# Regrouping the tokens of a fused agent-attention and feed-forward kernel: 26 pairs of 480-token groups become 24 pairs of 512 and one pair of 192

## The chip, the cores and the metric

The kernel runs on one core of one Trainium2 chip. A core has a matrix engine (TensorE, PE in the profile; its weight loads are PEld), a vector engine (VectorE, DVE), a scalar engine (ScalarE, ACT), GpSimd (POOL) and a queue engine that issues transfers (SyncE, SP). The metric is the device time of one execution in microseconds (us), lower is better.

## The reference, cut to what matters

```python
B, N, C = 2, 12480, 128;  n_agents = 49;  d_ff = 2048
def sm(a, b):                                   # softmax over b's rows
    s = (a @ b.T) / sqrt(C); e = exp(s - s.max(-1)); return e / (e.sum(-1) + 1e-9)
agent_v = sm(agents, k) @ v                     # per batch: 49 x 128
x = sm(q, agents) @ agent_v                     # per batch: 12480 x 128
h = x @ w_in                                    # 24960 x 2048
out = (max(h, 0) + alpha * min(h, 0)) @ w_out   # 24960 x 128
```

All data are float32 (the weights arrive as float64 words, which the kernel narrows).

## The kernel before, in words

The kernel never forms `x`. For each batch it folds `agent_v @ w_in` into one table `sab` (a high part `sa` and a low part `sb`, 49 agents padded to 64 rows, kept twice, once in each half of the 128 partitions) and works with the unnormalized softmax weights `qmh` + `qml` (high and low part) of each query. A product of two float32 values is built of three float32r passes (high with low, low with high, high with high).

`PReLU(h)` is split into a linear part and a ReLU part: the ReLU part runs over all 2048 columns of `d_ff`, and the linear part `alpha * h @ w_out` is folded into a 128 x 128 matrix `wz`, and with `agent_v` into `zh` + `zl` per batch.

**Groups and steps.** Tokens are taken in groups of GT = 480, 26 per batch, 52 in all. A group has NM = 8 steps, each of 256 columns of `d_ff`, so there are 416 steps. Step s consists of
- `g1`: h = sab.T @ (qmh, qml), 6 matmuls of 64 rows and 480 columns into one of two PSUM buffers; then on ScalarE `rh = relu(h)` and on VectorE `rl = max(h, 0) - rh`;
- `g2`: acc += wl.T rh + wh.T rh + wh.T rl, 12 matmuls of 64 rows and 480 columns.

Each matmul uses one half of the array's rows (`TILES`, rows 0 to 63 or 64 to 127), and the two halves work side by side, each in its own order. I call the time that one half takes for one matmul a *slot*: a step is 9 slots. After the last step of a group come three linear passes with `zh` and `zl` (line 854), one on the first half and two on the second, and then `os` (ScalarE copies one half of acc, VectorE adds the other), `ot` (a transposition on VectorE), `ot` times `qr` (the softmax denominators) and the store, 8 steps later.

**What sets the order.** The whole order is written out: at step s the loop (line 1118) emits first what `pre` put there, then `g1(s + 2)`, then what `at` put there, then `g2(s)`. Each engine works through its own list in that order. So `g1(s + 2)` may start only when `rl(s)` has freed the PSUM buffer, and everything that stands on VectorE ahead of an `rl` delays it.

**Beside the steps** runs, for each pair of groups, the query chain `q_chain` (load, transposition, split in high and low, logits `lg` of 6 slots, maximum over the agents on GpSimd, exponential, split, `qsum` of 2 slots, reciprocal). And while the first batch's groups run, the second batch's keys and values are worked off: `k_transpose_dve`, `k_logits` (`kl`, matmuls of 49 columns), `k_max_keys`; then `k_exp_a` (line 507, VectorE), `k_exp_b` (ScalarE), `k_exp_c` (line 526, VectorE), `v_split` (line 498, VectorE), `k_av2` (`av`, matmuls of 258 columns) and `k_add` (line 582, VectorE); and then `fold_tasks`: `den`, `avt`, four tasks `ta` (`a_ps`, 512 columns of `sab` each; one float32 matmul leaves two records), `tz` and `ts`, which make `zh` and `zl`. Their places are found by a planner: `fit` looks for a step in which the sum of VectorE or ScalarE costs stays under `ROOM` (1.4 and 1.1), and `hold` for one in which the misc PSUM buffer is free. A prologue of some 86 us does the first batch's keys and values and narrows the weights.

Of the kernel before, what the change touches and what calls it, by code (L numbers as in the profile page):

```python
# [20 lines left out]
ROOM = {"dve": 1.4, "act": 1.1}  # L21
# [4 lines left out]
SLAB_PARTS = (0, 0, 0, 1, 2, 3, 5, 6, 7, 10)  # L26
# [5 lines left out]
def kernel(  # L32
# [19 lines left out]
    GT = 480  # L52
    TB = GT // 32
    NG = N // GT
    KT = 512
# [10 lines left out]
    assert N % GT == 0 and N % 64 == 0 and NA <= HALF and C == P and D == P and DFF % W == 0  # L66
# [194 lines left out]
    def narrow_wo(n):  # L261
# [328 lines left out]
    def fold_tasks(b):  # L590
# [38 lines left out]
        def ta(n):  # L629
            def f():  # L630
                t = pair_tile(f"a_ps{b}_{n}", 0 if b == 0 and n == 1 else None)[:, 0, :]
                sl = slice(n * W, (n + 1) * W)
                nc.tensor.matmul(t, lhsT=w["avt"], rhs=win[:, sl], start=True, stop=True)
                nc.scalar.copy(out=w["sa"][:, sl], in_=t)
                nc.vector.tensor_tensor(
                    out=w["sb"][:, sl], in0=t, in1=w["sa"][:, sl], op=ALU.subtract
                )

            return f
# [13 lines left out]
        first = [t1, t2] + [ta(n) for n in range(4)]  # L653
# [45 lines left out]
    NGT = B * NG  # L699
    gq = {}  # L700

    def q_load(k):
        t = p2.tile([P, 2, TB, 32], F32, tag="qin", name=f"qin{k}")
        for i in range(2):
            b, r0 = (2 * k + i) // NG, (2 * k + i) % NG * GT
            view = q[b, r0 : r0 + GT, :].rearrange("(t j) (h b i) -> h b j t i", j=32, h=2, b=2)
            for h in range(2):
                for c in range(2):
                    p0 = HALF * i + 32 * c
                    nc.sync.dma_start(out=t[p0 : p0 + 32, h], in_=view[h, c])  # L710
        gq["in", k] = t
# [16 lines left out]
    def q_lo(k):  # L728
        t = p1.tile([P, 2, GT], F32R, tag="ql", name=f"ql{k}")
# [30 lines left out]
    def q_exp_hi(k):  # L760
        m = p2.tile([P, 2, GT], F32R, tag="qmh", name=f"qmh{k}")
# [7 lines left out]
    def q_split(k):  # L769
        m = p2.tile([P, 2, GT], F32R, tag="qml", name=f"qml{k}")  # L770
# [29 lines left out]
    def q_rec(k):  # L800
        t = p1m.tile([P, 32], F32, tag="qst", name=f"qst{k}")
        nc.vector.transpose(out=t, in_=gq.pop(("sum", k)))
        r = p2.tile([P, 2, TB, 1], F32, tag="qr", name=f"qr{k}")
        nc.vector.tensor_scalar(
            out=r.rearrange("p h t o -> p (h t o)"), in0=t[:, 0 : 2 * TB], scalar1=1e-9, scalar2=None, op0=ALU.add
        )
        nc.vector.reciprocal(out=r, in_=r)
        for i in range(2):
            gq["r", 2 * k + i] = r[:, i]
# [4 lines left out]
    def g1(s):  # L814
        g, m = divmod(s, NM)
        w, (mh, ml) = st[g // NG], gq["M", g]
        h = ps_h.tile([P, 2, 512], F32, tag="h", name=f"h{s}")
# [3 lines left out]
        for n, (a, x) in enumerate(jobs):  # L821
            for u, (r0, r1) in enumerate(TILES):
                f0 = (2 * m + u) * P
                nc.tensor.matmul(  # L824
                    h[:, u, 0:GT], lhsT=w[a][r0:r1, f0 : f0 + P], rhs=x[r0:r1, :],
                    start=n == 0, stop=n == 2,
                )
        rh = p3.tile([P, 2, GT], F32R, tag="rh", name=f"rh{s}")
        rl = p3.tile([P, 2, GT], F32R, tag="rl", name=f"rl{s}")
        nc.scalar.activation(out=rh, in_=h[:, :, 0:GT], func=AF.Relu)  # L830
        nc.vector.scalar_tensor_tensor(  # L831
            out=rl, in0=h[:, :, 0:GT], scalar=0.0, in1=rh, op0=ALU.max, op1=ALU.subtract
# [3 lines left out]
    def g2(s):  # L836
        g, m = divmod(s, NM)
        w = st[g // NG]
# [321 lines left out]
```

## Time and profile before

| what | value |
|---|---|
| median of 3 runs | 1036.88 us (1036.82 to 1041.66) |
| the profiled execution | 1039.85 us |
| its span, first to last instruction | 1038.1 us |
| TensorE busy / weight loads busy | 98% / 90% |
| VectorE / ScalarE / GpSimd busy | 79% / 61% / 11% |
| granted TensorE clock, mean | 0.994 of full speed |

The profiled execution took 1.75 us more than its span. A busy TensorE is not one that streams without gaps: records of two matmuls overlap, so the pace is read from the distance of their starts. The span has four stages: the prologue to 88.8 us, the keys of the second batch to 339.9 us, its values and the fold to 606.6 us, and then only groups and query chains.

### The profile page before, as it was taken

The page shows a single profiled execution, that of the slowest core. Times are in us where ns is not written, and L with a number is a line of the kernel's source. Part 1 is how long each engine was busy: PE and PEld are TensorE (multiplying, and loading weights), DVE is VectorE, ACT ScalarE, POOL GpSimd, SP SyncE. Part 2 cuts the span into 40 slices and gives each one's busy share as a digit, 9 for nine tenths or more (in the row PEclk, how much of TensorE's full clock was granted, in tenths as well). Part 3 has the DMA queues.
Part 4 walks back from the last instruction along what each step waited for, and adds up shares of the span by engine and source line. Part 5 has one row for each costly group of instructions (what it writes and reads, how often), then busy time and mean ns, then how long its engine had stood idle before and what let it go on. Part 6 is the DMA issues. An engine that isn't in the chain of part 4 may idle for free.

```text
span 1038.1 us, 22309 instructions
## 1 busy us (share of the span) xinstructions
PE 1018.8 (98%) x9263; PEld 936.6 (90%) x9263; DVE 818.6 (79%) x1040; ACT 630.8 (61%) x801; POOL 114.7 (11%) x138
## 2 busy tenths in 40 slices
PE   8999999999999999999999999999999999999997
PEld 7877888988999898999988799999999999999996
DVE  6776778878878899988976777787778877887775
ACT  4365656656655676776755666666656665666563
POOL 2260111011011011011011011101110011101100
PEclk9899999999999999999999999999999999999999
DMA  9963124333331232332210211121112120211011
GB/s 298 289 131 50 21 46 67 51 51 61 51 56 30 61 71 51 75 76 63 52 31 11 39 30 26 25 40 30 33 18 39 31 36 16 39 30 21 12 20 30
DMA packets 295045, 57.22 MB, mean 55 GB/s; under 512 B 265567, under 2 KB 292769, under 8 KB 294945
## 3 DMA queue, kind: packets, MB, share of 16 engines
q1 hardware_dynamic: 293953, 55.69, 26.8%
q8 instruction: 72, 1.18, 0.5%
q10 hardware_dynamic: 992, 0.12, 0.1%
q14 instruction: 28, 0.23, 0.1%
HBM read 42.59 MB, written 12.78 MB: 53 GB/s over the span
## 4 chain that ended last, share of the span: by engine, by line
PE 79%; DVE 13%; ACT 3%; DMA 3%; issue 2%; SPq 1%; DVEq 0%; ACTq 0%
PE acc L846 44%; PE h L824 23%; DVE rl L831 4%; PE lg L740 3%; PE kl L384 3%; ACT rh L830 2%; PE av L539 2%; PE acc L854 2%; DVE qt L718 1%; PE qsum L782 1%; DVE mx L423 1%; DVE ql L730 1%; DMA qin<-in_q_dram 1%; DMA win<-in_moe_w_in_dram 1%; DMA v<-in_v_dram 1%
## 5 line engine op out<-in xcount | busy, mean ns | idle before, releaser
L831 DVE SCALAR_TENSOR_TENSOR rl<-h,rh 128x960 fp32r<-128x960 f32 x416 | 478.7, 1152 | 186.5 <-ACT rh L830 182.9
L830 ACT ACTIVATE rh<-h 128x960 fp32r<-128x960 f32 x416 | 404.7, 973 | 286.8 <-PE h L824 277.8
L824 PE MATMUL h<-qmh,sab 64*128 64x480 f32 x1664 | 446.7, 381 | 4.1 <-DVE rl L831 3.3
L846 PE MATMUL acc<-rh,wl 64*128 64x480 f32 x1664 | 442.9, 380 | 1.2 <-DVE zl L649 0.7
L846 PE MATMUL acc<-rh,wh 64*128 64x480 f32 x1664 | 440.4, 377 | 0.0
L846 PE MATMUL acc<-rl,wh 64*128 64x480 f32 x1664 | 369.5, 378 | 0.0
L824 PEld LDWEIGHTS h<-qmh,sab 64*128 64x128 f32 x1664 | 252.2, 184 | 22.4 <-DVE rl L831 9.3
L846 PEld LDWEIGHTS acc<-rh,wl 64*128 64x128 f32 x1664 | 250.6, 184 | 17.1 <-issue 3.8
L846 PEld LDWEIGHTS acc<-rh,wh 64*128 64x128 f32 x1664 | 251.8, 184 | 10.2
L846 PEld LDWEIGHTS acc<-rl,wh 64*128 64x128 f32 x1664 | 247.3, 184 | 11.5
L824 PE MATMUL h<-qml,sab 64*128 64x480 f32 x832 | 254.3, 377 | 0.0
L753 POOL PARTITION_ALL_REDUCE qm<-qs x26 | 79.6, 3063 | 716.2 <-ACT qs L748 696.3
L824 PEld LDWEIGHTS h<-qml,sab 64*128 64x128 f32 x832 | 134.2, 185 | 4.8
L859 ACT COPY os<-acc 128x480 f32<-128x480 f32 x52 | 29.1, 560 | 40.8 <-PE acc L854 40.8
L384 PEld LDWEIGHTS kl<-ag,kt 64*128 64x128 f32 (+2 forms) x588 | 50.8, 193 | 2.2 <-ACT s L513 0.6
L384 PE MATMUL kl<-ag,kt 64*128 64x49 f32 (+2 forms) x588 | 51.4, 272 | 0.2 <-ACT kt L356 0.2
L860 DVE TENSOR_TENSOR os<-acc,os 128x480 f32<-128x480 f32 x52 | 33.6, 646 | 2.4 <-ACT os L859 2.4
L725 ACT CAST qh<-qt 128x960 fp32r<-128x960 f32 x26 | 25.9, 997 | 14.5 <-DVE qt L718 14.5
L865 DVE STREAM_TRANSPOSE ot<-os 128x480 f32<-128x480 f32 x52 | 34.7, 666 | 0.0
L870 DVE TENSOR_TENSOR ot<-ot,qr 128x480 f32<-128x480 f32 x52 | 33.6, 647 | 0.0
L404 ACT COPY s<-kl 128x196 f32<-128x196 f32 (+2 forms) x38 | 14.1, 370 | 29.0 <-PE kl L384 29.0
L748 ACT COPY qs<-lg 128x960 f32<-128x960 f32 x26 | 25.0, 960 | 10.4 <-PE lg L740 10.4
(148 smaller groups left out, 894.6 us busy)
## 6 DMA issues: line engine op xcount, KB each, us to landing
qin<-in_q_dram SPq DMA_DIRECT2D x208, 60.0 KB, 2.2
out_dram<-ot SPq DMA_DIRECT2D x206, 60.0 KB, 1.9
v<-in_v_dram SPq DMA_DIRECT2D x12, 512.0 KB, 8.0
kb<-in_k_dram SPq DMA_DIRECT2D x96, 64.0 KB, 2.2
v<-in_v_dram SPq DMA_DIRECT2D x24, 256.0 KB, 2.8
k<-in_k_dram SPq DMA_DIRECT2D x11, 512.0 KB, 8.4
win<-in_moe_w_in_dram SPq DMA_DIRECT2D x4, 512.0 KB, 8.0
wo<-in_moe_w_out_dram SPq DMA_DIRECT2D x4, 512.0 KB, 9.5
```

Of the source, the lines that this page charges most:

```text
L384: nc.tensor.matmul(d[0:rows, c : c + NA], lhsT=kt[r0:r1, n * rows : (n + 1) * rows], rhs=st[b]["ag"][r0:r1, 0:NA], start=True, stop=True,)
L725: nc.scalar.copy(out=t, in_=gq["t", k])
L740: nc.tensor.matmul(t[:, i, 0:GT], lhsT=a[r0:r1, h].rearrange("p d a -> p (d a)"), rhs=x[r0:r1, h, :], start=n == 0, stop=n == len(jobs) - 1,)
L753: nc.gpsimd.partition_all_reduce(flat(t), flat(gq["s", k]), P, ReduceOp.max)
L824: nc.tensor.matmul(h[:, u, 0:GT], lhsT=w[a][r0:r1, f0 : f0 + P], rhs=x[r0:r1, :], start=n == 0, stop=n == 2,)
L830: nc.scalar.activation(out=rh, in_=h[:, :, 0:GT], func=AF.Relu)
L831: nc.vector.scalar_tensor_tensor(out=rl, in0=h[:, :, 0:GT], scalar=0.0, in1=rh, op0=ALU.max, op1=ALU.subtract)
L846: nc.tensor.matmul(acc[:, i, 0:GT], lhsT=a[r0:r1, 2 * m + u, :], rhs=x[r0:r1, u, :], start=m == 0 and n == 0, stop=False,)
L859: nc.scalar.copy(out=t, in_=acc[:, 0, 0:GT])
L860: nc.vector.tensor_tensor(out=t, in0=acc[:, 1, 0:GT], in1=t, op=ALU.add)
L865: nc.vector.transpose(out=t.rearrange("p t i -> p (t i)"), in_=oo.pop(g))
L870: nc.vector.tensor_tensor(out=t, in0=t, in1=gq.pop(("r", g)).to_broadcast([P, TB, 32]), op=ALU.mult)
```

## The change

Groups have 512 tokens: 24 per batch, 48 in all. The 192 tokens that are left of each batch are two more groups, which form one last pair (the first of that pair belongs to batch 0, the second to batch 1). There are 50 groups and 400 steps instead of 416: 384 of 512 columns and 16 of 192. Tiles are cut to each pair's width by `pair_of`.

The three linear passes of a group put two on the second half for even groups, as before, and two on the first half for odd ones.

The second batch's keys start 3 steps earlier (`base + 5`), the planner's limits are 1.46 and 1.15, and its work has to be done in 16 steps fewer, since the first batch has 192 steps instead of 208. The four `ta` of the second batch become two tasks of two. In the prologue the tasks of `narrow_wo` move by a step (`SLAB_PARTS`) and `part` has one buffer.

```diff
-ROOM = {"dve": 1.4, "act": 1.1}
+ROOM = {"dve": 1.46, "act": 1.15}
-SLAB_PARTS = (0, 0, 0, 1, 2, 3, 5, 6, 7, 10)
+SLAB_PARTS = (0, 0, 0, 1, 2, 3, 5, 7, 7, 9)
...
-    GT = 480
+    GT = 512
     NG = N // GT
+    REST = N - NG * GT
...
-            part = x["part"] = p_tmp.tile([P, q4, D], F32, tag="part", name=f"part{n}", bufs=2)
+            part = x["part"] = p_tmp.tile([P, q4, D], F32, tag="part", name=f"part{n}", bufs=1)
...
-        def ta(n):
+        def ta(*ns):
...
+                for t, n in enumerate(ns):
+                    sl = slice(n * W, (n + 1) * W)
+                    nc.tensor.matmul(
+                        ps[:, t, :], lhsT=w["avt"], rhs=win[:, sl], start=True, stop=True
+                    )
+                    nc.scalar.copy(out=w["sa"][:, sl], in_=ps[:, t, :])
...
-        first = [t1, t2] + [ta(n) for n in range(4)]
+        whole = [(0, 1), (2, 3)] if b else [(n,) for n in range(4)]
+        first = [t1, t2] + [ta(*ns) for ns in whole]
...
-    NGT = B * NG
+    groups = [(b, g * GT, GT) for b in range(B) for g in range(NG)]
+    groups += [(b, NG * GT, REST) for b in range(B)]
+    NGT = len(groups)
...
+    def pair_of(pool, tag, k, dt=F32):
+        n = groups[2 * k][2]
+        t = pool.tile([P, 2 * GT], dt, tag=tag, name=f"{tag}{k}")[:, 0 : 2 * n]
+        return t.rearrange("p (h n) -> p h n", h=2)
...
-            for i, a, x in ((0, "zh", mh), (1, "zl", mh), (1, "zh", ml)):
+            jobs = ((0, "zh", mh), (1, "zl", mh), (1, "zh", ml))
+            if g % 2:
+                jobs = ((0, "zl", mh), (1, "zh", mh), (0, "zh", ml))
+            for i, a, x in jobs:
...
-            at(base + 8, k_begin, b, [(0, NU)], parts)
-            s = base + 9
+            at(base + 5, k_begin, b, [(0, NU)], parts)
+            s = base + 6
```

What moves is shown at three places. In all three, `name<-names` is what a row writes and reads; numbers after a name are the step, group or pair, then the buffer.

**First place: VectorE, where `zl` of the second batch stands** (`ot` is the scaling of an output group, `os` its sum, `rl` the step's own work). Before:

```order
L831 SCALAR_TENSOR_TENSOR rl209_7930<-h209_7922,rh209_7929 128x960
L870 TENSOR_TENSOR ot24_7760<-ot24_7760,qr12_7787 128x480
L649 TENSOR_TENSOR zl1_7935<-z_ps1_7908,zh1_7934 128x128
L860 TENSOR_TENSOR os25_7953<-acc25_7734,os25_7953 128x480
L831 SCALAR_TENSOR_TENSOR rl210_7964<-h210_7956,rh210_7963 128x960
```

And now:

```order
L853 SCALAR_TENSOR_TENSOR rl200_7666<-h200_7658,rh200_7665 128x1024
L774 TENSOR_TENSOR qs13_7573<-qs13_7573,qm13_7586 128x1024
L853 SCALAR_TENSOR_TENSOR rl201_7692<-h201_7684,rh201_7691 128x1024
L897 TENSOR_TENSOR ot23_7523<-ot23_7523,qr11_7309 128x512
L654 TENSOR_TENSOR zl1_7697<-z_ps1_7670,zh1_7696 128x128
L886 TENSOR_TENSOR os24_7715<-acc24_7499,os24_7715 128x512
L853 SCALAR_TENSOR_TENSOR rl202_7726<-h202_7718,rh202_7725 128x1024
```

Before, `zl1` stood ahead of the sum of group 25, the last group of the first batch, which does not read it; the first group that reads it, group 26, ended 8 steps later. Now it stands ahead of the sum of group 24, which is the first group of the second batch and reads it.

**Second place: VectorE at the values of the second batch** (steps 124 to 126; `qst`, `qr` reciprocal of the denominators, `s1` is `k_exp_a`, `e2` is `k_exp_c`, `v2` is `v_split`, `x1` is `k_add`). Before:

```order
L831 SCALAR_TENSOR_TENSOR rl124_5079<-h124_5071,rh124_5078 128x960
L802 STREAM_TRANSPOSE qst7_5082<-qx7_4893 128x32
L804 TENSOR_SCALAR qr7_5084<-qst7_5082 128x30
L807 RECIPROCAL qr7_5084<-qr7_5084 128x30
L507 TENSOR_TENSOR s1_1363<-s1_1363,kmax1_1365 128x196 x2
L582 TENSOR_TENSOR x1_1366<-av1_2_5097,x1_1366 98x516
L831 SCALAR_TENSOR_TENSOR rl125_5142<-h125_5134,rh125_5141 128x960
L771 TENSOR_TENSOR qml8_5145<-qs8_4824,qmh8_5049 128x960
L526 TENSOR_TENSOR e2_1_4_5114<-s1_1363,e2_1_4_5114 128x4x49
L831 SCALAR_TENSOR_TENSOR rl126_5174<-h126_5166,rh126_5173 128x960
```

And now:

```order
L853 SCALAR_TENSOR_TENSOR rl124_5081<-h124_5073,rh124_5080 128x1024
L822 STREAM_TRANSPOSE qst7_5084<-qx7_4893 128x32
L824 TENSOR_SCALAR qr7_5086<-qst7_5084 128x32
L828 RECIPROCAL qr7_5086<-qr7_5086 128x32
L526 TENSOR_TENSOR e2_1_4_5054<-s1_1284,e2_1_4_5054 128x4x49
L498 TENSOR_TENSOR v2_1_5_5117<-v1_5_4877,v2_1_5_5117 128x4x128
L582 TENSOR_TENSOR x1_1287<-av1_2_5099,x1_1287 98x516
L853 SCALAR_TENSOR_TENSOR rl125_5145<-h125_5137,rh125_5144 128x1024
L787 TENSOR_TENSOR qml8_5148<-qs8_4822,qmh8_5050 128x1024
L526 TENSOR_TENSOR e2_1_5_5121<-s1_1284,e2_1_5_5121 128x4x49
L853 SCALAR_TENSOR_TENSOR rl126_5179<-h126_5171,rh126_5178 128x1024
```

Here a `v2` and an `e2` moved into a step that had two `s1`; at step 126 the values are one block further on than before.

**Third place: TensorE, where `sab` of the second batch is made** (`a_ps` is `ta`). Before:

```order
L824 MATMUL h192_7427<-qml12_7357,sab0_1049 128x480 x2
L824 MATMUL h192_7427<-qmh12_7286,sab0_1049 128x480 x2
L633 MATMUL a_ps1_0_7440<-win_89,avt1_7387 128x512
L846 MATMUL acc23_7262<-rh190_7378,wl_95 128x480 x2
L846 MATMUL acc23_7262<-rh190_7378,wh_94 128x480 x2
```

And now:

```order
L846 MATMUL h190_7365<-qml11_6856,sab0_1049 128x512 x2
L846 MATMUL h190_7365<-qmh11_6762,sab0_1049 128x512 x2
L635 MATMUL a_ps1_0_7378<-win_89,avt1_7325 128x512 x2
L869 MATMUL acc23_7256<-rh188_7303,wl_95 128x512 x2
L869 MATMUL acc23_7256<-rh188_7303,wh_94 128x512 x2
```

Four interruptions by one matmul of the whole array became two by two matmuls.

## Rows read from the trace of the kernel before

**Rows 1.** The page, busy time, share of the span and instructions of each engine.

```profile
PE 1018.8 (98%) x9263; PEld 936.6 (90%) x9263; DVE 818.6 (79%) x1040; ACT 630.8 (61%) x801; POOL 114.7 (11%) x138
```

**Rows 2.** Three stages: stretch, length, busy time and count per engine, clock, DMA.

```profile
88.80:339.90 251.10, 249.23 (x2410) 221.39 (x2408) 198.17 (x236) 145.27 (x163) 21.78 (x14) 1.00 0.29 47
339.90:606.60 266.70, 263.32 (x2414) 232.05 (x2414) 226.39 (x307) 178.63 (x243) 25.19 (x40) 1.00 0.25 52
606.60:1014.10 407.50, 407.50 (x3715) 399.62 (x3713) 314.27 (x347) 254.79 (x274) 34.34 (x23) 1.00 0.17 28
```

**Rows 3.** Timeline of ScalarE, last stage, one row per pair of groups: start, length.

```profile
723.46 1.00 ACT L725 CAST qh<-qt 128x960 fp32r<-128x960 f32 x1 [0.51 <-DVE qt L718]
...
757.52 1.00 ACT L725 CAST qh<-qt 128x960 fp32r<-128x960 f32 x1 [0.51 <-DVE qt L718]
```

**Rows 4.** Timeline of TensorE at the end of a group, two linear passes.

```profile
710.87 0.37 PE L854 MATMUL acc<-qmh,zl 64*128 64x480 f32 x1
...
711.08 0.37 PE L854 MATMUL acc<-qml,zh 64*128 64x480 f32 x1
```

**Rows 5.** Timeline of TensorE, 512-column matmuls in the prologue, all eight and the first two.

```profile
64.33 2.11 PE L160 MATMUL stoke_max<-wh 128*128 128x512 f32 x8
...
64.33 0.73 PE L160 MATMUL stoke_max<-wh 128*128 128x512 f32 x2
```

**Rows 6.** Timeline of TensorE, narrower matmuls of 64 rows.

```profile
159.41 1.97 PE L384 MATMUL kl<-ag,kt 64*128 64x49 f32 x31
...
431.62 0.64 PE L572 MATMUL av<-v,e 64*98 64x258 f32 x8
```

**Rows 7.** Weight loads by line, 100 to 1000 us: count, busy, mean ns, idle before.

```profile
L824 PEld LDWEIGHTS h<-qmh,sab 64*128 64x128 f32 x1587 | 240.1, 184 | 18.3 <-DVE rl L831 8.5
...
L384 PEld LDWEIGHTS kl<-ag,kt 64*128 64x128 f32 x384 | 24.5, 187 | 0.3
```

**Rows 8.** VectorE by line, 339.9 to 606.6 us: count, busy, mean ns, idle before.

```profile
L831 DVE SCALAR_TENSOR_TENSOR rl<-h,rh 128x960 fp32r<-128x960 f32 x113 | 130.3, 1153 | 40.5 <-ACT rh L830 39.7
L498 DVE TENSOR_TENSOR v<-v,v 128x512 fp32r<-128x512 f32 x24 | 16.1, 672 | 0.0
...
L526 DVE TENSOR_TENSOR e<-s,e 128x196 fp32r<-128x196 f32 x24 | 9.2, 400 | 0.0
...
L507 DVE TENSOR_TENSOR s<-s,kmax 128x196 f32<-128x196 f32 x24 | 7.6, 348 | 0.0
L582 DVE TENSOR_TENSOR x<-av,x 98x516 f32<-98x516 f32 x11 | 7.5, 686 | 0.0
```

**Rows 9.** Waits, 111.5 to 606.6 us: who for whom, us, times, longest.

```profile
PEld h L824 <- DVE rl L831: 8.5, 15, 1.0
```

**Rows 10.** Timeline: the last step's chain, and a `zl` early in the span.

```profile
1026.85 0.38 PE L824 MATMUL h<-qmh,sab 64*128 64x480 f32 x1
...
1027.27 0.98 ACT L830 ACTIVATE rh<-h 128x960 fp32r<-128x960 f32 x1 [1.00 <-PE h L824]
...
1028.28 1.16 DVE L831 SCALAR_TENSOR_TENSOR rl<-h,rh 128x960 fp32r<-128x960 f32 x1 [0.81 <-ACT rh L830]
...
106.56 0.28 DVE L649 TENSOR_TENSOR zl<-z_ps,zh 128x128 fp32r<-128x128 f32 x1
```

**Rows 11.** Timeline of TensorE around one `ta` of the second batch.

```profile
565.82 0.37 PE L824 MATMUL h<-qmh,sab 64*128 64x480 f32 x1
566.12 1.12 PE L633 MATMUL a_ps<-win,avt 128*128 128x512 f32 x2
...
567.49 0.38 PE L846 MATMUL acc<-rh,wh 64*128 64x480 f32 x2
```

**Rows 12.** Timeline of the end, after the last matmul.

```profile
1031.64 0.56 ACT L859 COPY os<-acc 128x480 f32<-128x480 f32 x1 [3.40 <-PE acc L854]
...
1032.23 0.66 DVE L860 TENSOR_TENSOR os<-acc,os 128x480 f32<-128x480 f32 x1 [2.23 <-ACT os L859]
...
1033.64 0.66 DVE L870 TENSOR_TENSOR ot<-ot,qr 128x480 f32<-128x480 f32 x1
```

More of the change, by code (lines that the diff above doesn't have):

```diff
@@ L627, in t2 @@
             w["sa"], w["sb"] = t[:, 0:DFF], t[:, DFF : 2 * DFF]
-        def ta(n):
+        def ta(*ns):
             def f():
[L631 to L637, printed above, removed]
+                i = 0 if b == 0 and ns == (1,) else None
+                ps = pair_tile(f"a_ps{b}_{ns[0]}", i)
+                for t, n in enumerate(ns):
[4 more added lines that the diff above has]
+                    nc.scalar.copy(out=w["sa"][:, sl], in_=ps[:, t, :])
+                    nc.vector.tensor_tensor(
+                        out=w["sb"][:, sl], in0=ps[:, t, :], in1=w["sa"][:, sl],
+                        op=ALU.subtract,
+                    )
             return f
@@ L800, in q_rec @@
     def q_rec(k):
+        nb = groups[2 * k][2] // 32
         t = p1m.tile([P, 32], F32, tag="qst", name=f"qst{k}")
         nc.vector.transpose(out=t, in_=gq.pop(("sum", k)))
[L803 removed]
+        r = p2.tile([P, 32, 1], F32, tag="qr", name=f"qr{k}")[:, 0 : 2 * nb, :]
         nc.vector.tensor_scalar(
[L805 removed]
+            out=r.rearrange("p t o -> p (t o)"), in0=t[:, 0 : 2 * nb], scalar1=1e-9,
+            scalar2=None, op0=ALU.add,
         )
@@ L837, in g2 @@
         g, m = divmod(s, NM)
-        w = st[g // NG]
+        b, _, n = groups[g]
+        w = st[b]
         if m == 0:
-            oo[g] = pair_tile(f"acc{g}", g % 2)
+            oo[g] = pair_tile(f"acc{g}", g % 2)[:, :, 0:n]
         acc = oo[g]
@@ L843, in g2 @@
         jobs = [(wl, rh, 0), (wh, rh, 0), (wl, rh, 1), (wh, rh, 1), (wh, rl, 0), (wh, rl, 1)]
-        for n, (a, x, u) in enumerate(jobs):
+        for j, (a, x, u) in enumerate(jobs):
             for i, (r0, r1) in enumerate(TILES):
                 nc.tensor.matmul(
-                    acc[:, i, 0:GT], lhsT=a[r0:r1, 2 * m + u, :], rhs=x[r0:r1, u, :],
-                    start=m == 0 and n == 0, stop=False,
+                    acc[:, i, :], lhsT=a[r0:r1, 2 * m + u, :], rhs=x[r0:r1, u, :],
+                    start=m == 0 and j == 0, stop=False,
                 )
@@ L870, in o_scale @@
         nc.vector.tensor_tensor(
-            out=t, in0=t, in1=gq.pop(("r", g)).to_broadcast([P, TB, 32]), op=ALU.mult
+            out=t, in0=t, in1=gq.pop(("r", g)).to_broadcast(list(t.shape)), op=ALU.mult
         )
@@ L875, in o_store @@
     def o_store(g):
+        b, r0, n = groups[g]
         t = oo.pop(("n", g))
-        dst = out[g * GT : (g + 1) * GT, :].rearrange("(t j) (b i) -> b j t i", j=32, b=4)
+        rows = out[b * N + r0 : b * N + r0 + n, :]
+        dst = rows.rearrange("(t j) (b i) -> b j t i", j=32, b=4)
         for i in range(4):
```

107 lines of the change are left out of this document (57 added, 50 removed).

## The prediction

> **What bounds the kernel now.** I read the busy line first [rows 1]: TensorE is busy 98% of the span, VectorE 79%. A share of busy time is an average, so the three stages come next [rows 2]. From 606.6 us on TensorE is busy in all of 407.5 us and, by the list of waits, waits for nobody. There a matmul saved is time saved, and nothing done on VectorE counts. From 88.8 to 606.6 us the list of waits has 8.5 us of TensorE waiting for `rl` [rows 9]; there VectorE's order counts too. The granted clock is 1.00 in all three stages, which is the 2.4 GHz level.
>
> The unit is the slot, the time of one matmul on one half of the array. In the last stage two `qh` stand 34.06 us apart [rows 3]; that is one pair of groups. The half with two linear passes works off 16 x 9 + 2 x 2 passes + 6 `lg` + 2 `qsum` = 156 matmuls in it, so a slot of 480 columns is 34.06 / 156 = 0.2183 us. Two linear passes in a row on one half stand 0.21 apart [rows 4]: they are worked off one after the other, and the other half, with 154 matmuls, has to idle for two slots in each pair or run ahead.
>
> **The change part by part.** *Width.* At 2.4 GHz 32 more columns take 32 / 2400 = 0.0133 us, so a slot of 512 columns is 0.2317. Two rows bound it. Matmuls of 512 columns on the whole array took (2.11 - 0.73) / 6 = 0.230 each [rows 5]; if the slot grew in proportion to its columns, it would be 0.2183 x 512 / 480 = 0.2329. I take 0.2317, as the part of a slot that isn't streaming (0.2183 - 480 / 2400 = 0.018) has no reason to grow with the columns.
>
> *The narrow pair.* No row has 192 columns. From below there is streaming plus the same fixed part, 0.080 + 0.018 = 0.098. Matmuls of 49 columns, 31 on two halves in 1.97 us [rows 6], took between 1.97 / 16 = 0.123 and, less one record of at most 0.37 [rows 4], (1.97 - 0.37) / 15 = 0.107; so few columns don't go below that. Those of 258 columns, 8 in 0.64, took 0.120 if the record of the last one is 0.28 (0.37 less 222 columns of streaming): (0.64 - 0.28) / 3. As 192 lies between 49 and 258, I take 0.115.
>
> *Balance.* With the passes alternating, both halves have 155 matmuls per pair. A pair of 1024 tokens takes 155 x 0.2317 = 35.91 us.
>
> *Together*, for TensorE alone: 26 x 34.06 = 885.56 before; 24 x 35.91 + 155 x 0.115 = 861.92 + 17.83 = 879.75 now. That is **-5.8 us**. Nearly all of it is the balance, one slot in each of 26 pairs (5.7); what the wider groups save in fixed parts, the narrow pair takes back. While the first batch's groups run, the waits of rows 9 bring the halves together anyway, so I count half the balance there (13 pairs x 0.2183 / 2): **+1.4**.
>
> *The merged `ta`.* Without it the second matmul behind the `h` of 565.82 would start two slots later, at 566.26; it starts at 567.49 [rows 11]. An interruption costs 1.23 us, of which the matmul itself is 1.12, so that only the 0.1 or so around it is saved: two in four, **-0.3** with their extra slack (between 0 and -1).
>
> *The new wait for `zl`.* `zl1` now stands on VectorE behind `rl201` and `ot23` (first place). The linear passes of group 24 read it, and on TensorE they come 7 slots (one of `h`, six of `g2(199)`) behind the start of the last `h201`: 7 x 0.2317 = 1.62 us. VectorE's way to `zl1` from that same start is: 0.42 to the start of `rh`, 0.98 for it, 0.03, 1.16 for `rl`, 0.28 for `zl` [rows 10], 0.66 for `ot` [rows 12], and for 64 and 32 more columns 0.13 (the slopes, from 480 to 960 columns, are 0.00088 us on ScalarE and 0.00103 on VectorE [rows 8, 10, 12]). That is 3.66. TensorE stands still for 3.66 - 1.62 = **+2.0** (1.6 to 2.4). Behind the waiting pass stand the matmuls of `h202`, behind these `rh202` and `rl202`, and `os24`; nothing in the order hides it. Before, `zl` stood where no group in work needed it: 0.
>
> *The values in fewer steps.* From step 114 to 131 the order gives VectorE two `v`, two `s`, three `e` and one `x` more than the same steps had: 2 x 0.672 + 2 x 0.348 + 3 x 0.400 + 0.686 = 3.9 us [rows 8]. Width adds 18 x 0.09 = 1.6 (`rl` 0.066, the rest query chain and output). TensorE, in 18 x 9 slots, gets 2.2 us longer, and the `av` matmuls moved there take 1.0. VectorE is worse off by 3.9 + 1.6 - 3.2 = 2.3; later steps (152 to 163) add 1.2 in the same way. Of 3.5 us I let 40% show, **+1.5**, because VectorE has 40 us of idle time in that stage [rows 8], and only what lands ahead of an `rl` that TensorE already waits for is lost (rows 9: 8.5 us over 500 us). It is -0.5 if the new places (second place: two `s` gone, a `v` and an `e` in) break up bunches instead, +3.5 if all shows. The keys start three steps earlier in the same sequence: VectorE gets 0.12 us more a step, and TensorE 0.12: 0.
>
> *The narrow steps.* From the last `h` to the end of `rl` it takes, with 576 columns less, 0.42 - 0.12 + (0.98 - 0.51) + 0.03 + (1.16 - 0.59) = 1.37 us; TensorE comes back to that buffer after 16 slots x 0.115 = 1.84. That cover of 0.47 per step holds alone, but `os` and two `ot` of 0.66 - 0.30 = 0.36 each stand between: up to 1.1 - 0.47 in a bunch, and the first bunch is that of a 512 group. **+0.5** (0 to 2.5).
>
> *End and beginning.* After the last matmul one operation on ScalarE and three on VectorE have 288 columns less: 0.25 + 3 x 0.30 = **-1.1** [rows 12]. In the prologue two VectorE and two ScalarE operations of the first query chain are 64 columns longer: **+0.25**. `SLAB_PARTS` and the single `part` buffer leave VectorE the same `narrow_wo` operations, which it works off one behind the other as before, so the order itself covers the single buffer: 0; if one of them is caught ahead of the first `rl`, it is about one operation of 512 columns, 0.67 [rows 8].
>
> **The sum.** -5.8 + 1.4 - 0.3 + 2.0 + 1.5 + 0.5 - 1.1 + 0.25 = -1.55. The profiled execution took 1039.85 us, 1.75 more than its span; with the change 1038.3. It stands 2.97 above the median of the runs shown, 1036.88, and I take the same distance: **1035.3 us**.
>
> **A rule of the skill beside a row.** Weight loads of fp32r took 184 ns, those of the fp32 matmuls of 49 columns 187 ns [rows 7]: no difference by type. The Trainium skill, "TensorE: Matmul & The Clock Gate", section "Weight-path perf modes — Fast Weight Load (FWL) and DoubleRow", says that the fast weight load is on whenever there are 128 weights and the type is not FP32. By that rule the fp32r matmuls here would load fast, and what holds up narrow matmuls in fp32 would not hold them. By it the sum would be 1032.7 us, by the row it stays at 1035.3 (the last rival has the working); the trace speaks against the rule.
>
> **The rivals.** *A cheaper slot.* If the slot of 512 columns is that of rows 5, 0.230, then 24 x 155 x 0.0017 = 6.3 us go; with the whole balance in the first batch too (1.4) the time is 1027.6. For it: the row is of this very width. Against: it is the prologue, on the whole array, where no half has to share with the other.
>
> *Loads as a floor, the slower side.* TensorE's loads are busy 90% [rows 1]; one of 184 ns hides behind a slot of 218 but not behind one of 115. If a half can't start its next load while one runs, a narrow slot is 0.184, and the pair costs 155 x 0.069 = 10.7 more: 1046.0. From a floor of 0.15 it decides. Against: the 49-column matmuls ran at most 0.123 apart while their loads took 187 [rows 6, 7], so loads overlap there.
>
> *A slot in proportion to its columns*, 0.2329: 24 x 155 x 0.0012 = +4.5, 1039.8, slower than before. Two rows of different width in one form would tell; there are none.
>
> *The change doesn't do what it says.* If the halves don't drift and the balance is worth nothing in the last stage either, the other 4.3 us are missing: 1039.6. Against: 156 slots of 0.2183 account for the pair, and two passes stand in series [rows 4].
>
> *Fast loads.* If the narrow fp32r slot goes to its streaming bound, 0.098, the pair saves 155 x 0.017 = 2.6: 1032.7. Rows 7 speak against it. (It is the Trainium skill's rule above.)
>
> **How the numbers follow.** A measurement of this kernel can tell about 0.5%, 5.2 us, from no change. Forecast 0.49, cheaper slot 0.24, loads as a floor 0.10, proportional slot 0.09, no balance 0.05, fast loads 0.03. The forecast's own range, from its open terms (values -2 to +2, narrow steps -0.5 to +2, first batch's balance and `ta` +-1.5), is 1031.5 to 1039.5. Both rivals near 1039.7 and most of the cheaper slot have to be in, the floor is left out: 1028 to 1043. Faster than 1031.7: the cheaper slot and 0.04 of the forecast, 0.28. Slower than 1042.1: the floor and 0.03 of the proportional slot with late values, 0.13. The rest, 0.59, is within.
>
> **What the profile after would show.** Two `qh` of the last stage 35.9 us apart (35.65: cheaper slot; 36.1: proportional; 36.15: no balance). The narrow steps 9 x 0.115 = 1.04 us each (0.88 with fast loads, 1.66 with a floor). One wait of about 2 us of `acc` for `zl` near step 200; if there is none, that term falls. The waits of `h` for `rl` at about 10 us, up from 8.5. From the last matmul to the end 1.1 us less than before. Wrong it would be made above all by the slot: each thousandth of a microsecond is 3.7 us; next by stalls of the halves on each other that no list of waits names.

## The result and the profile after

The changed kernel took 1052.54 us (median of 5, 1048.73 to 1061.23) where the kernel before took 1036.88 (median of 5): 1.0147 times as long, 95% interval 1.0113 to 1.0182. Forecast were 1035.3 us and a range of 1028 to 1043; the kernel is slower, and the time lies outside the range. Single executions of either kernel spread over some 12 us with their mean granted clock (0.984 to 0.999 for before). In the kept traces that clock differs in the prologue (0.74 to 1.00 from 20 to 40 us); from 90 us to the last matmul it is 1.00 but for the waits described below. So where a few us matter, executions of the same mean clock are compared, or the time from the first `rl` to the end of the span, which the prologue doesn't touch.

The profiled execution of the changed kernel took 1051.68 us, its span is 1049.9, against 1039.85 and 1038.1. Its first `rl` starts at 91.77 us (88.78 before), and from there to the end it takes 958.1 us (949.3 before): 3.0 us more in the prologue and 8.8 behind it. The page's busy line and its TensorE clock (the span in 40 slices, tenths of full speed), which answer to [rows 1]:

```profile
PE 1022.7 (97%) x8953; PEld 905.1 (86%) x8953; DVE 815.3 (78%) x1011; ACT 626.8 (60%) x778; POOL 113.1 (11%) x112
...
PEclk9899999999999999999999899999999999999999
```

There is a slice in the middle with the clock below 0.9 that the page of before does not have:

```profile
PEclk9899999999999999999999999999999999999999
```

Three stretches that answer to the stages of [rows 2] (the first is shorter, it begins 24 us behind the first `rl`), and the waits of TensorE and of its weight loads in the first two (us in total, times, longest):

```profile
115.50:356.50 241.00, 238.41 (x2232) 198.48 (x2228) 194.31 (x220) 141.41 (x150) 20.60 (x7) 1.00 0.31 50
356.50:631.00 274.50, 264.60 (x2259) 212.15 (x2257) 224.65 (x295) 176.26 (x233) 22.55 (x32) 0.99 0.25 51
631.00:1009.40 378.40, 378.40 (x3261) 373.00 (x3259) 290.44 (x302) 235.15 (x241) 33.67 (x11) 1.00 0.17 28
```

```profile
PE a_ps L635 <- DVE sab L639: 6.3, 2, 3.2
PE h L846 <- DVE rl L853: 4.6, 10, 0.6
PE acc L880 <- DVE zl L654: 1.4, 1, 1.4
```

```profile
PEld h L846 <- DVE rl L853: 13.1, 22, 1.0
```

In the second stage TensorE is idle for 274.50 - 264.60 = 9.9 us, where it was 3.4 in [rows 2]. The new row is the first of the waits: `a_ps` waited for VectorE's subtraction `sab`, twice, for 3.1 and 3.2 us. The third row is the wait that was forecast, for `zl`. Here is the first of the two `ta` tasks in order of time, TensorE (which answers to [rows 11]) and then VectorE:

```profile
571.58 0.40 PE L846 MATMUL h<-qmh,sab 64*128 64x512 f32 x2
571.91 1.13 PE L635 MATMUL a_ps<-win,avt 128*128 128x512 f32 x2
576.25 1.13 PE L635 MATMUL a_ps<-win,avt 128*128 128x512 f32 x2 [3.21 <-DVE sab L639]
577.31 0.62 PE L869 MATMUL acc<-rh,wl 64*128 64x512 f32 x2
577.73 0.63 PE L869 MATMUL acc<-rh,wh 64*128 64x512 f32 x2
578.15 0.63 PE L869 MATMUL acc<-rh,wl 64*128 64x512 f32 x2
```

```profile
572.12 1.22 DVE L787 TENSOR_TENSOR qml<-qs,qmh 128x1024 fp32r<-128x1024 f32 x1
573.25 1.22 DVE L853 SCALAR_TENSOR_TENSOR rl<-h,rh 128x1024 fp32r<-128x1024 f32 x1
574.38 1.23 DVE L735 STREAM_TRANSPOSE qs<-qin 128x1024 f32<-128x1024 f32 x1
575.54 0.65 DVE L639 TENSOR_TENSOR sab<-a_ps,sab 128x512 fp32r<-128x512 f32 x1
```

The merged task writes matmul, copy, subtraction, and then the second matmul. ScalarE's copy of the first half is done at 573.66, but the subtraction stands on VectorE behind `qml`, `rl` and a transposition, starts at 575.54 and ends at 576.19. Only then the second matmul of the same task starts. Every matmul of the steps stands behind it. What follows is slow too: the matmuls of the steps start 0.42 us apart instead of 0.23, and a table of short stretches shows why (length, busy time and count per engine in the order of [rows 2], then the granted clock, the DMA share and GB/s):

```profile
575.00:578.00 3.00, 1.75 (x6) 0.89 (x8) 1.20 (x2) 0.59 (x1) 0.00 (x0) 0.92 0.00 0
578.00:580.00 2.00, 2.00 (x12) 1.53 (x12) 0.69 (x1) 0.00 (x0) 0.00 (x0) 0.50 0.00 0
580.00:582.00 2.00, 2.00 (x16) 1.59 (x14) 0.00 (x0) 0.68 (x1) 0.00 (x0) 0.76 0.00 0
582.00:584.00 2.00, 2.00 (x14) 1.05 (x10) 1.23 (x1) 1.86 (x3) 0.00 (x0) 1.00 0.00 0
584.00:588.00 4.00, 0.89 (x2) 0.30 (x2) 2.96 (x3) 1.00 (x2) 0.00 (x0) 0.97 0.00 0
588.00:592.00 4.00, 4.00 (x18) 2.22 (x18) 0.69 (x1) 0.59 (x1) 0.00 (x0) 0.60 0.01 4
```

Behind each idle stretch the granted clock falls to 0.50, the level of 1.2 GHz; by the matmuls that start 0.42 us apart it stays there for some 3 us. The page's slice with an 8 is this place.

The last stage has no such trouble. Two `qh`, which answer to [rows 3], and steps of the narrow pair on TensorE:

```profile
664.95 1.05 ACT L740 CAST qh<-qs 128x1024 fp32r<-128x1024 f32 x1 [0.51 <-DVE qs L735]
701.04 1.05 ACT L740 CAST qh<-qs 128x1024 fp32r<-128x1024 f32 x1 [0.52 <-DVE qs L735]
```

```profile
1033.80 0.28 PE L846 MATMUL h<-qmh,sab 64*128 64x192 f32 x2
...
1034.81 0.28 PE L846 MATMUL h<-qmh,sab 64*128 64x192 f32 x2
...
1035.81 0.27 PE L846 MATMUL h<-qmh,sab 64*128 64x192 f32 x2
```

A pair of groups takes 36.09 us (forecast 35.91), which is 155 slots of 0.2328. A narrow step takes 1.005, nine slots of 0.1117.

### The profile page after: what moved, and what is told of

Read it like the earlier page. It is cut to its first block, busy times and chain, and to the rows that moved or that the text cites. A ratio compares the mean times of both kernels' runs of the same rounds, so it can differ in the third digit from the quotient of the medians.

```text
span 1049.9 us, 21503 instructions
## 1 busy us (share of the span) xinstructions
PE 1022.7 (97%) x8953; PEld 905.1 (86%) x8953; DVE 815.3 (78%) x1011; ACT 626.8 (60%) x778; POOL 113.1 (11%) x112
## 3 DMA queue, kind: packets, MB, share of 16 engines
q8 instruction: 70, 1.15, 0.4%
## 4 chain that ended last, share of the span: by engine, by line
PE 78%; DVE 15%; ACT 4%; issue 2%; DMA 1%; SPq 0%; DVEq 0%; ACTq 0%
PE acc L869 43%; PE h L846 22%; DVE rl L853 5%; PE lg L756 3%; PE kl L384 3%; ACT rh L852 2%; PE av L539 2%; DVE qs L735 1%; PE acc L880 1%; DVE ql L745 1%; PE qsum L799 1%; DVE mx L423 1%; DVE kt L366 1%; DVE ot L897 1%; DVE v L498 1%
## 5 line engine op out<-in xcount | busy, mean ns | idle before, releaser
L853 DVE SCALAR_TENSOR_TENSOR rl<-h,rh 128x1024 fp32r<-128x1024 f32 (+1 forms) x400 | 476.4, 1192 | 193.8 <-ACT rh L852 189.4
L852 ACT ACTIVATE rh<-h 128x1024 fp32r<-128x1024 f32 (+1 forms) x400 | 402.1, 1005 | 294.4 <-PE h L846 288.5
L846 PE MATMUL h<-qmh,sab 64*128 64x512 f32 (+1 forms) x1600 | 408.2, 390 | 5.5 <-DVE rl L853 4.6
L869 PE MATMUL acc<-rh,wl 64*128 64x512 f32 (+1 forms) x1600 | 407.2, 390 | 0.0
L869 PE MATMUL acc<-rh,wh 64*128 64x512 f32 (+1 forms) x1600 | 406.9, 390 | 0.0
L869 PE MATMUL acc<-rl,wh 64*128 64x512 f32 (+1 forms) x1600 | 323.3, 388 | 0.0
L846 PE MATMUL h<-qml,sab 64*128 64x512 f32 (+1 forms) x800 | 230.6, 386 | 0.0
L886 DVE TENSOR_TENSOR os<-acc,os 128x512 f32<-128x512 f32 (+1 forms) x50 | 33.3, 666 | 3.2 <-ACT os L885 3.2
L892 DVE STREAM_TRANSPOSE ot<-os 128x512 f32<-128x512 f32 (+1 forms) x50 | 34.4, 687 | 0.0
L740 ACT CAST qh<-qs 128x1024 fp32r<-128x1024 f32 (+1 forms) x25 | 25.7, 1028 | 13.7 <-DVE qs L735 13.7
L897 DVE TENSOR_TENSOR ot<-ot,qr 128x512 f32<-128x512 f32 (+1 forms) x50 | 33.4, 667 | 0.0
```

What stands on the lines that cost most here:

```text
L846: nc.tensor.matmul(h[:, u, :], lhsT=w[a][r0:r1, f0 : f0 + P], rhs=x[r0:r1, :], start=j == 0, stop=j == 2,)
L852: nc.scalar.activation(out=rh, in_=h, func=AF.Relu)
L853: nc.vector.scalar_tensor_tensor(out=rl, in0=h, scalar=0.0, in1=rh, op0=ALU.max, op1=ALU.subtract)
L869: nc.tensor.matmul(acc[:, i, :], lhsT=a[r0:r1, 2 * m + u, :], rhs=x[r0:r1, u, :], start=m == 0 and j == 0, stop=False,)
L886: nc.vector.tensor_tensor(out=t, in0=acc[:, 1, :], in1=t, op=ALU.add)
L892: nc.vector.transpose(out=t, in_=oo.pop(g))
```

## The experiments

**The matmuls of the merged `ta` first.**

```diff
                 for t, n in enumerate(ns):
                     sl = slice(n * W, (n + 1) * W)
                     nc.tensor.matmul(...)
+                for t, n in enumerate(ns):
+                    sl = slice(n * W, (n + 1) * W)
                     nc.scalar.copy(...)
```

> The changed kernel, with the two matmuls of a merged ta written one behind the other ahead of the four copies and subtractions. Theory: the second matmul waited for the subtraction of the first half only because both halves lie in one tile and the subtraction stood ahead of it in the code. Then the waits of a_ps for sab (3.2 and 3.1 us in the trace of the changed kernel) go, and with them the low clock behind each (eight slots at 0.42 instead of 0.233 us, and a second matmul that took 0.7 us longer): 6.3 + 1.5 + 1.7 = 9.5 us off the changed kernel's 1052.5, 1043.0; the granted clock from 570 to 600 us is 1.00. Rival: the copies are late anyhow, the wait moves to the next user of that PSUM buffer, and less than 3 us go. A second rival: the waits go and the clock drops stay: 6.3 us go.

It took 1041.84 us (1.0034 times before, 0.9995 to 1.0072), 10.7 less than the changed kernel by the medians of two series. The stretches from 570 us on:

```profile
570.00:576.00 6.00, 6.00 (x40) 3.76 (x38) 5.22 (x5) 2.36 (x3) 0.00 (x0) 1.00 0.10 16
576.00:582.00 6.00, 6.00 (x40) 3.73 (x40) 4.48 (x6) 3.96 (x5) 0.00 (x0) 1.00 0.01 3
582.00:588.00 6.00, 6.00 (x56) 4.92 (x54) 4.64 (x6) 4.07 (x5) 0.00 (x0) 1.00 0.16 28
588.00:594.00 6.00, 6.00 (x54) 4.92 (x52) 3.42 (x4) 3.15 (x4) 2.41 (x1) 1.00 0.09 16
```

TensorE is busy throughout and the clock stays at 1.00. From the first `rl` to the end the kernel takes 948.1 us instead of 958.1: 10.0 us, close to the 9.5 expected. The waits and the low clock go together; the theory holds, both rivals fall.

The same run has two more waits that bear on the cause, both on ScalarE:

```profile
571.72 1.98 PE L635 MATMUL a_ps<-win,avt 128*128 128x512 f32 x4
573.74 0.59 ACT L640 CAST sab<-a_ps 128x512 fp32r<-128x512 f32 x1 [0.88 <-PE a_ps L635]
576.04 0.59 ACT L640 CAST sab<-a_ps 128x512 fp32r<-128x512 f32 x1 [1.71 <-DVE sab L641]
```

The first copy reads only the half that the first matmul writes. In the changed kernel it started right behind that matmul (573.07, the matmul ended at 573.04). Here it starts behind both (they end at 573.70), though ScalarE stood idle for 0.88 us. The second copy waits for VectorE's subtraction of the first half, though the two share no column, only their tiles.

**The merged `ta` alone in the kernel before**, written as the change writes it (`whole = [(0, 1), (2, 3)]` for the second batch).

> The kernel before with the merged ta alone, as the change writes it (matmul, copy, subtraction, and then the second matmul). Theory: two waits of a_ps for sab of 3 us each and the low clock behind them, some 9 to 10 us in all, less one interruption of 0.1 to 0.3 us twice: 1046. Rival: the wait came from the tight order of the changed kernel, and here it is under 2 us in all: 1037 to 1039.

It took 1045.06 us against 1038.73 in the same series (1.0078, 1.0048 to 1.0108), and the two profiled executions have spans of 1047.4 and 1038.1. From the first `rl` (89.0 and 88.8 us) to the end that is 958.4 against 949.3: 9.1 us. The waits and two stretches of it:

```profile
PE a_ps L635 <- DVE sab L639: 5.8, 2, 2.9
```

```profile
574.00:578.00 4.00, 2.05 (x4) 0.55 (x4) 1.90 (x3) 0.00 (x0) 0.00 (x0) 0.67 0.00 0
578.00:582.00 4.00, 4.00 (x21) 3.35 (x22) 0.69 (x1) 0.58 (x1) 0.00 (x0) 0.50 0.00 0
```

So the wait has nothing to do with the width or the 16 steps fewer. The rival falls: this one part of the change, alone, costs some 9 us, most of the whole loss. The medians give less (6.3), the fastest executions of the two (1044.75 and 1035.74 us) 9.0.

**The linear passes as before** in the changed kernel (the two lines with `if g % 2` taken out).

> The changed kernel with the linear passes as before, two on the second half in every group. Pair of groups in the last stage, 36.08 us with the passes alternating. Theory A (the balance is worth one slot a pair, and a slot of 512 columns is 0.2328, in proportion to its columns): 156 x 0.2328 = 36.31, the kernel 24 x 0.23 = 5.6 us slower than the changed one. Theory B (the slot is 0.2317 when the halves are out of step and 0.0011 longer in step): 156 x 0.2317 = 36.15, 1.6 us slower. Theory C (the balance is worth nothing): 36.08, no difference.

The median, 1052.95 us, is too near the changed kernel's to tell; the 5.6 us of theory A are not there. From the first `rl` to the end it takes 960.9 us against 958.1, 2.8 more. The pairs are exact; in the last stage and while the keys run:

```profile
172.75 1.05 ACT L740 CAST qh<-qs 128x1024 fp32r<-128x1024 f32 x1 [0.34 <-DVE qs L735]
213.15 1.05 ACT L740 CAST qh<-qs 128x1024 fp32r<-128x1024 f32 x1 [0.34 <-DVE qs L735]
...
700.28 1.05 ACT L740 CAST qh<-qs 128x1024 fp32r<-128x1024 f32 x1 [0.52 <-DVE qs L735]
736.59 1.05 ACT L740 CAST qh<-qs 128x1024 fp32r<-128x1024 f32 x1 [0.52 <-DVE qs L735]
```

In the last stage a pair takes 36.31, as theory A has it to the hundredth: the balance is worth one slot, and a slot of 512 columns is 0.2328 balanced or not. While the keys run it takes 40.40, and so it does in the changed kernel (`qh` at 173.92 and 214.32): there the balance is worth nothing. Over the some 11 pairs of the last stage that is 11 x 0.22 = 2.4 us.

**The alternating passes alone in the kernel before.**

> The kernel before with the alternating passes alone. Pair in the last stage 34.06 us before. Theory A (balance is worth a slot, slots as they are): 155 x 0.2183 = 33.84; over 26 pairs up to 5.7 us, 1031.2 if all counts, 1032.6 if half counts in the first batch. Theory B (halves in step cost 0.0011 a slot): 155 x 0.2194 = 34.01, 1.3 us at most. Theory C (worth nothing): 34.06, no difference.

```profile
163.96 1.00 ACT L725 CAST qh<-qt 128x960 fp32r<-128x960 f32 x1 [0.34 <-DVE qt L718]
202.24 1.00 ACT L725 CAST qh<-qt 128x960 fp32r<-128x960 f32 x1 [0.35 <-DVE qt L718]
...
719.96 0.99 ACT L725 CAST qh<-qt 128x960 fp32r<-128x960 f32 x1 [0.51 <-DVE qt L718]
753.80 0.99 ACT L725 CAST qh<-qt 128x960 fp32r<-128x960 f32 x1 [0.51 <-DVE qt L718]
```

A pair of the last stage takes 33.84 (34.06 in [rows 3]), again as theory A says; while the keys run it takes 38.28, and before it took that too (`qh` at 166.84 and 205.12). The medians, 1036.33 against 1036.97 (0.999, 0.9957 to 1.0023), can't tell 2.4 us; from the first `rl` to the end it takes 946.8 us against 949.3, 2.5 less, not the 5.7 that theory A gave with all 26 pairs counted or the 4.3 with half of the first batch. At a mean clock of 0.997 the executions took 1034.3 to 1034.5, those of before 1036.7 to 1036.9.

**Groups of 384**, read only for the slot (`GT = 384`, matmuls of `ta` first).

> The changed kernel, matmuls of ta first, with groups of 384 tokens (32 per batch and the same narrow pair), read only for its slot. A pair in the last stage has 155 matmuls a half. Slot in proportion to its columns: 0.2183 x 384 / 480 = 0.1746, a pair of 27.07 us. A fixed part of 0.018 and streaming at 2.4 GHz: 0.178, a pair of 27.6. If loads of 184 ns hold a slot up, 0.184 or more, 28.5 or more; if VectorE is the bound there, TensorE waits for rl and the matmuls in between tell the slot.

```profile
699.52 0.84 ACT L742 CAST qh<-qs 128x768 fp32r<-128x768 f32 x1 [0.52 <-DVE qs L737]
726.72 0.84 ACT L742 CAST qh<-qs 128x768 fp32r<-128x768 f32 x1 [0.52 <-DVE qs L737]
```

TensorE waits for nobody in the last stage there. A pair takes 27.20, a slot 27.20 / 155 = 0.1755; the kernel took 1050.29 us in its one execution. With 0.2183 at 480 and 0.2328 at 512 the slope is (0.2328 - 0.1755) / 128 = 0.00045 us a column, and what is left at no columns is 0.1755 - 384 x 0.00045 = 0.003. The fixed part of 0.018 that the prediction took is not there.

**The prologue's part of the change alone in the kernel before** (the new `SLAB_PARTS`, `part` with one buffer).

> The kernel before with the prologue's part of the change alone: the new SLAB_PARTS and one part buffer. In the traces so far the first rl starts at 88.8 (before) and 85.9 us (before with alternating passes, the same prologue), and at 91.8, 91.6, 90.6 us in three kernels with the changed prologue. Theory: the one part buffer makes ScalarE and VectorE wait on each other in the prologue, and the first rl comes 2 to 4 us later, near 90; the time is 1039 to 1041. Rival: the start varies by that much from one execution to the next whatever the code, and the time is within 1 us of before at the same granted clock.

It took 1040.45 us against 1038.73 (1.0029, 0.9997 to 1.006). At a mean clock of 0.997 it is 1039.0 to 1039.8 against 1036.8: 2 to 3 us. One of ScalarE's casts of `part` into `wh`, then two stretches of the prologue, and the first of them in the kernel before:

```profile
64.72 0.62 ACT L276 CAST wh<-part 128x512 fp32r<-128x512 f32 x1 [3.80 <-DVE part L270]
```

```profile
60.00:70.00 10.00, 6.64 (x42) 4.75 (x42) 8.50 (x17) 3.68 (x11) 4.14 (x7) 0.97 0.89 178
70.00:80.00 10.00, 9.53 (x77) 8.21 (x78) 4.06 (x11) 5.51 (x16) 5.23 (x5) 0.86 0.00 0
```

```profile
60.00:70.00 10.00, 9.02 (x63) 7.19 (x62) 8.56 (x19) 6.69 (x21) 5.93 (x11) 1.00 0.58 141
```

ScalarE's cast waits 3.80 us for `part` (0.18 before), TensorE is busy 6.64 us of ten where it was 9.02, and from 70 to 80 us the clock is 0.86 where it was 1.00. The changed kernel shows the same (3.80 us, and 0.83 there). The first `rl` of this run starts at 88.6 us, though, not near 90, and no later than before (88.8), and behind it everything takes as long as before (949.2 and 949.3 us). The rival is right in part: with one and the same old prologue it started at 85.9 and at 88.8, and the clock from 20 to 40 us was 0.91 and 0.74 in those two. At 0.91 the old prologue ends at 85.9 and 85.8 in two kernels, the new one (with the wider tiles too) at 89.5 and 90.6 in two others; this run needed 88.6 at a clock of 1.00. So the new prologue is not free: 2 to 3 us alone, some 4 in the wide kernel at the same clock. Whether the single buffer or the new `SLAB_PARTS` costs it no run takes apart.

**`zl` one step earlier** in the kernel with the matmuls of `ta` first (`at(s, rest[1])` for `at(s + 1, rest[1])`).

> The changed kernel with the matmuls of ta first (1041.8 us), and zl made one step earlier, ahead of rl201. There the passes of group 24 waited 1.4 us for zl (1.7 us by the weight loads), and the step lost 1.95 us in all against its matmuls. Theory: the wait goes and nothing else is late there: 1.4 to 1.9 us off, 1040.2. Rival: acc of the next group or os24, which stands behind, is late as well, and under 0.7 us go.

1038.48 us, 3.4 less than without it by the medians; at a mean clock of 0.996 to 0.997 1036.4 to 1037.5 against 1039.4 to 1039.6; from the first `rl` to the end 946.1 against 948.1. TensorE waits for nothing from 520 to 620 us. So the wait for `zl` was real, and it cost 2 us.

**Groups of 480 with all that proved worth keeping**: alternating passes, merged `ta` with its matmuls first, `zl` a step earlier.

> Groups of 480 tokens as before, with what the runs so far found worth keeping: alternating passes, the merged ta with its matmuls first, zl made ahead of the next rl. Between the last two stages the changed kernel with these repairs lost 2.35 us against its matmuls (groups 22 to 25), before 4.62 (groups 23 to 26). Theory: the alternation is worth 0.19 us in each pair of the last stage (12 pairs, 2.3 us), the fold 2.3 more; 4.6 us off before at the same granted clock, pairs of 33.87 us. And the same kernel in 512 groups (1036.4 at a clock of 0.997) should be 4 to 6 us slower than this: 2.5 from the prologue, the rest from 24 x 155 x 0.2328 + 17.4 = 883.4 us of matmuls against 26 x 155 x 0.2185 = 880.6. Rival: width is worth something after all, and the two are within 2.5 us, the prologue's share. A second rival: the repairs of the fold do nothing at 480, where zl stood one group earlier: only 2.3 us off before.

```profile
718.06 1.00 ACT L733 CAST qh<-qt 128x960 fp32r<-128x960 f32 x1 [0.51 <-DVE qt L726]
751.93 1.00 ACT L733 CAST qh<-qt 128x960 fp32r<-128x960 f32 x1 [0.51 <-DVE qt L726]
```

1033.76 us against 1037.18, 0.9964 (0.9932 to 0.9995): faster than both kernels, though by 0.4% only. At a mean clock of 0.996 four executions took 1032.6 to 1034.5, two of before 1036.8 and 1038.9: some 4 us. From the first `rl` to the end it takes 945.1 us, 4.2 less than before and 1.7 less than with the alternation alone, so the repairs of the fold count at 480 as well and the second rival falls. The repaired kernel in 512 groups is 4.7 us slower by the medians of two series, 2 to 5 at the same clock, and 4.7 by the two spans. Of these 3.7 lie ahead of the first `rl` (85.84 and 89.51 us, the clock from 20 to 40 us being 0.91 in both), and only 1.0 behind it: the theory has the size, but not the split of 2.5 and 2.8, and the first rival falls. The matmuls are 2.9 us dearer in the wide kernel (883.5 against 26 x 33.87 = 880.6), its end 1.3 cheaper. That the width brings something is excluded by the pairs.

## Why the prediction was wrong

Point by point, the forecast's sum against what the runs showed:

| term | forecast | measured | from |
|---|---|---|---|
| merged `ta` | -0.3 | +10.0 | its repair, 958.1 - 948.1; alone at 480 +9.1 |
| matmuls, with the balance | -5.8 | -2.1 | 24 x 36.09 + 155 x 0.1117 = 883.5 against 885.6 |
| balance in the first batch | +1.4 | +2.6 | 12 pairs x 0.22, of which nothing shows |
| prologue | +0.25 | +3.0 | first `rl` at 88.78 and 91.77 us |
| `zl` | +2.0 | +0.3 | 2.0 by its repair, less the 1.7 that the fold of before lost as well (946.8 - 945.1) |
| values in fewer steps, narrow steps | +1.5 and +0.5 | -0.6 together | what the 1.0 us between the two repaired kernels leaves: 1.0 - 2.9 + 1.3 |
| end | -1.1 | -1.3 | 6.5 us from the last `os` before, 5.2 now |

The column adds up to 11.9 us, and the two spans are 11.8 apart. Its rows are differences of single traces, good to a few tenths. For the profiled execution 1038.3 us were forecast and 1051.68 measured: of these 13.4 us the merged `ta` is 10.3 and the prologue 2.75. The remaining 3.8 of the 17.2 us by the medians are the distance between profiled execution and median, 2.97 above it before and 0.86 below it now: a matter of which executions were taken, not of the change.

All the other terms together are -1.2 us (948.1 - 949.3) where -1.5 was forecast. That is luck: matmuls and balance came out 4.9 us dearer than the sum had them, the waits for `zl`, the values and the narrow steps 4.3 us cheaper.

**The step that failed** is the merged `ta`. The working took each `ta` as one interruption of 1.23 us, of which the matmul is 1.12, and let merging save the rest. It had shown, in the third place of the order, two `a_ps` matmuls one behind the other on TensorE and went no further. But an order of one engine says nothing of what an instruction waits for. The code says it: between the two matmuls the changed `ta` writes a copy and a subtraction that read the same tile. That the second matmul waits for them though it writes the other half is what the runs show, and writing both matmuls first takes the wait away. That waits here are kept for a tile as a whole fits this and the two waits of ScalarE in the repaired kernel, where again only the tile is shared; how a wait comes to be set no trace shows. Unmerged tasks had no such wait: each took a new tile of the same buffer, but the planner kept them two steps or more apart (`hold`), and the readers were done by then. The subtraction then stands in VectorE's order behind operations of 1.2 us (`qml`, `rl` and a transposition at the first wait, `rl` and `ql` at the second), which is where a wait becomes 3 us. The prediction asked of every moved step who waits for it; for this one it asked only what its matmul costs.

The same step left out the clock. Each wait of 3 us was followed by some 3 us at 1.2 GHz, during which a slot took 0.42 us instead of 0.23 (at 577.31, 577.73 and 578.15 in the rows of the first `ta`). Eight such slots behind the first wait are 8 x 0.19 = 1.5 us; behind the second the `a_ps` matmul itself took 1.84 us instead of 1.13, and the slots behind it some 1 us more. With 6.3 in the list of waits that is 9.5, where the repair gave 10.0 and the experiment at 480 9.1.

**The slot** was the second error, 24 x 155 x 0.0011 = 4.1 us. Taking the granted clock of 1.00 for 2.4 columns a nanosecond left 0.018 us unexplained, and the prediction called that a fixed part, which a wider group would save. Its own rows spoke against it. The `av` matmuls of 258 columns took 0.120 [rows 6], and from there to 0.2183 at 480 the slope is 0.098 / 222 = 0.00044 us a column, which gives 0.2325 at 512. The prediction used that row for the narrow pair alone. The rival "slot in proportion to its columns" had a chance of 0.09 and gave 0.2329; it is the one that came true. With it, width saves nothing, and the narrow pair, at a floor of 0.112 where its share of the columns would be 0.087, costs 155 x 0.025 = 3.9 us.

**The floor.** The slower rival, weight loads as a floor of 0.184, fell: narrow slots take 0.1117, and 0.115 was forecast. So did the fast loads: the Trainium skill, "TensorE: Matmul & The Clock Gate", section "Weight-path perf modes — Fast Weight Load (FWL) and DoubleRow", excepts, of the types, only FP32 from the fast loads and does not name fp32r. If fp32r doesn't count as FP32, its loads should be fast, yet in the changed kernel they take 185 ns in the mean, those of the 49-column fp32 matmuls 188, and the narrow slot is 0.1117, not 0.098. What sets 0.1117 no run shows; from 1011 to 1043 us of the changed kernel weight loads are busy 31.94 of 32.00 us, so a shorter floor by the loads is not excluded.

**The balance** was right in the last stage to a hundredth of a us per pair, in both widths. In the first batch it is worth nothing, not half: a pair with the keys takes 40.40 us with and without it, presumably because the half with a pass less then only waits longer for `rl`. It fits that the waits of `h` for `rl` rise by 1.0 us with the alternation in both widths (3.3 to 4.3 at 480, 3.6 to 4.6 at 512); that this is the whole reason is argued, not shown.

**The new wait for `zl`** was right in its place and size: 1.4 us by the matmuls' list, 2.0 by its repair. (The sum's 0.13 for the wider operations should be 0.155, which changes nothing.) Only the "0 before" was wrong. Before, the list of waits has a matmul of `acc` that waits for `zl` once:

```profile
PE acc L846 <- DVE zl L649: 0.7, 1, 0.7
```

That matmul reads no `zl`. It is the first of the next group, and by the code its `acc` takes the PSUM buffer that held `z_ps`, from which `zl` is made. The prediction had asked only who reads `zl`, not who waits for its buffer.

**The prologue's** new order was costed at nothing with the cover "VectorE works these off one behind the other as before". The cover was named for the wrong engine: it is ScalarE's cast that waits 3.8 us for `part`, and behind it stand the exponentials of the prologue. The longest wait of TensorE's `av` matmuls there, for VectorE's `x`, went from 0.8 to 2.3 us.

**The values** cost less than forecast. The waits of `h` for `rl` did rise, from 8.5 [rows 9] to 13.1 us by the weight loads, which the prediction took for TensorE's waits, and from 3.3 to 4.6 by the matmuls themselves. But the alternation alone, at 480 and with the values where they were, already shows 9.8 and 4.3, and by the table the term is about nothing. So the longer waits in the list can't be taken for longer time.

## What to carry to other kernels

When two operations are merged into one task, look at what stands between them in the code and reads the same tile: write all the matmuls first, then the readers, since a wait of TensorE stands in front of everything that it does, and behind each wait of 3 us here the clock was at half for 3 more. Before counting on wider tiles, take the pace from two widths in the trace; one width and a nominal clock give a fixed part that need not be there. A term whose sign is sure should still be tried against the stage it falls in: the alternation gained a slot a pair where TensorE is the bound, and nothing where it waits for another engine anyway.

## What the runs showed of the hardware

Matmuls of 64 rows on two halves of the array at a granted clock of 1.00 took 0.1755, 0.2183 and 0.2328 us for 384, 480 and 512 columns: 2.2 columns a nanosecond with a fixed part of some 0.003 us. 192 columns took 0.1117, and 49 columns no less than 0.107. The Trainium skill, "TensorE: Matmul & The Clock Gate", section "Wait — 56ns, not 53.3ns?", gives N / 2.4 GHz and about 2.5 ns for matmuls in a row: the fixed part agrees, the rate does not. By that rule the slot of 512 columns would be an estimated 0.216; why it is 0.233 here no run explains.

Idle stretches of TensorE of about 3 us in the middle of dense work were each followed by some 3 us at half the clock; after a wait of 1.4 us (for `zl`) the granted clock stayed at 1.00, and the next matmuls ran at 0.23 us again after one interval of 0.34.

Operations that shared a tile but no column of it waited for each other: a matmul for the readers of the tile's other half (3.2 us), a copy for the matmul into the other half (0.88 us), and the next copy for the subtraction of the other half (1.71 us).
